# State kept in its PSUM bank, first MLP product in pairs of 64-row tiles, integer rounding in tables, last chunk in halves, new order: an RWKV-7 recurrence with Fourier mix and MLP on one core

## Chip, cores and metric

The kernel runs on one core of one Trainium2 chip. The metric is the device time of one execution in microseconds (us), median of several runs. A profiled execution gives the span from the first to the last instruction; in the profiles here it is 1.7 to 1.9 us shorter than the run that it belongs to. A run counts as slow if it took over 1.5% more than the fastest of the same kernel; comparisons use the others.

## The reference, cut to what matters

```python
# r, k, v, w, a, b: 4 batches x 8 heads x 768 steps x 40, float32
for t in range(S):
    y[:, :, t] = einsum('bhd,bhde->bhe', rt, state)
    Sa = einsum('bhde,bhe->bhd', state, at)
    state = state * wt[:, :, None, :] - einsum('bhd,bhe->bhde', Sa, bt) + einsum('bhd,bhe->bhde', vt, kt)
# x = y with the heads joined: 4 x 768 x 320
u   = x + real(fft(fft(x, axis=1), axis=2))
un  = (u - mean(u)) / sqrt(var(u) + 1e-6)
out = u + relu(un @ w_ch1) @ w_ch2          # 320 -> 1280 -> 320
```

The kernel walks the recurrence in 24 chunks of 128 steps (6 per batch). The Fourier mix and the MLP of one batch run beside the recurrence of the next.

## The kernel before

The kernel first records its operations (which buffers each reads and writes, on which engines it could run), then plays them in a fixed order, a string that was found offline: it fixes the sequence on each engine, the engine of each operation and the buffer slot of each result. At run time each engine takes its own list strictly in order and waits on semaphores. **So an operation that got faster can leave a gap where the order was made for a slower one.**

PSUM is held as four tiles of two banks each, and cut into eight one-bank slots:

```python
banks = [psum.tile([128, 1024], FP32, tag=f"ps{i}", name=f"ps{i}") for i in range(4)]
ps = Pool("ps", [banks[i // 2][:, i % 2 * 512:(i % 2 + 1) * 512] for i in range(8)], banks)
```

Some operations fill a whole two-bank tile. The framework tracks who must wait for whom by tile. Left alone, it would make a user of bank 5 wait for the users of bank 4. So the kernel declares, after each operation, that its instructions do not depend on those of the neighbouring bank, `b ^ 1`, except on true predecessors (`keep`):

```python
def part(self, banks, before=()):
    if len(banks) == 1:
        (b,) = banks
        keep = [i for o in before for i in o.made]
        for i in self.made:
            own = [n for n in ("PE", "Activation", "DVE") if n in str(i.engine)]
            for n in ("PE", "Activation", "DVE"):
                if n not in own:
                    self.tc.declare_no_dep(i, group=f"bank{b ^ 1}{n}", keep=keep, reason="another bank")
            self.tc.add_to_no_dep_group(f"bank{b}{own[0]}", i)
    ...
```

The first MLP product and the state update, as they ran (`NF` is 10 tiles of 128 hidden features; 320 rows make two and a half groups of 128, the last half is zeros):

```python
for m in range(0, NF):                       # PAIRED is empty in this kernel
    for kt in range(3):
        mm(o_, w1sb[:, kt, m * 128:(m + 1) * 128], unT()[:, :, kt], kt == 0)   # 128 rows, 384 columns
...
if st is not None and not held:              # HELD is empty: 16 such additions run
    nc.vector.tensor_add(Q(), Q(), st[0]())
...
nc.vector.tensor_tensor(s32(), Q(), decay(), Alu.mult)      # state to SBUF
```

## Time and profile before

| | before |
|---|---|
| time, median of 3 runs when the prediction was made | 237.38 us (237.0 to 238.84) |
| span of the profiled run, granted TensorE clock | 235.7 us, 0.998 |
| TensorE, VectorE, ScalarE, GpSimd busy | 95%, 88%, 77%, 65% |
| matmuls | 3664 |

The prediction below shows the head, the slices and the stretches. What it doesn't show is what TensorE waited for. The view of waits of the kernel before, of TensorE, gives for each line and releaser the us in total, the times, and the longest:

```profile
PE ps L160 <- DVE pr L160: 1.5, 3, 1.0
PE ps L160 <- DVE fill L160: 1.3, 1, 1.3
PE ps L160 <- DVE kb L160: 0.7, 1, 0.7
PE ps L160 <- DVE xs L160: 0.4, 2, 0.3
```

The reader is to see that these waits are few and short, that none names the result `h` of the MLP, and none names SyncE. The 1.3 us on `fill` is the start of the program.

### The profile page before, as it was taken

To read this page: it belongs to the slowest core of one execution; us is meant where nothing else is said; L and a number is where in the kernel's file an instruction comes from. 1 tells how busy PE (TensorE), PEld (TensorE's weight loads), DVE (VectorE), ACT (ScalarE), POOL (GpSimd) and SP (SyncE) were. 2 spreads that over 40 slices of the span, in tenths; PEclk is the share of its full clock that TensorE was granted. 3 is DMA by queue.
4 is the path that set the end of the run, shared out by engine and by line. 5 is a ranking of instruction groups with operands and counts; after the bars stand their busy time and mean duration, and the time that the engine had idled before them with its cause. 6 is when DMAs were issued, how large, how long until landed. Compare 5 with 4: busy or idle time off the path is not lost.

```text
span 235.7 us, 8993 instructions
## 1 busy us (share of the span) xinstructions
PE 224.1 (95%) x3664; PEld 170.7 (72%) x3664; DVE 208.0 (88%) x411; ACT 182.3 (77%) x378; POOL 153.5 (65%) x242
## 2 busy tenths in 40 slices
PE   7878999889999999999999999999999999999994
PEld 2446778678877777788867687888877787876662
DVE  6999999999999998998999999999899998689342
ACT  4879998798999899847799858968899895536240
POOL 6087998699999798458467267787979858200000
PEclk9999999999999999999999999999999999999999
DMA  7999889999999999999998899998999640002004
GB/s 121 185 171 188 152 147 165 158 158 167 182 173 173 144 163 158 169 148 156 180 209 196 151 188 167 164 158 151 222 196 191 114 104 3 3 0 86 0 34 160
DMA packets 171832, 33.93 MB, mean 144 GB/s; under 512 B 167120, under 2 KB 171472, under 8 KB 171792
## 3 DMA queue, kind: packets, MB, share of 16 engines
q1 hardware_dynamic: 170112, 31.73, 78.0%
q0 software_dynamic: 1680, 1.64, 4.3%
q8 instruction: 28, 0.46, 0.8%
q14 instruction: 12, 0.10, 0.2%
HBM read 26.87 MB, written 3.93 MB: 131 GB/s over the span
## 4 chain that ended last, share of the span: by engine, by line
PE 52%; DVE 16%; ACT 12%; issue 6%; DMA 5%; POOL 4%; SPq 3%; DVEq 0%; POOLq 0%; ACTq 0%
PE ps L160 52%; DVE pr L160 4%; SPq L433 3%; DVE xb L160 2%; POOL nat L472 2%; DMA in<-in_k_dram 2%; DMA in<-in_r_dram 2%; DVE xs L160 1%; DMA in<-in_w_dram 1%; DVE sm L160 1%; ACT kb L160 1%; DVE h L160 1%; ACT L160 1%; ACT tk L160 1%; DVE un L160 1%
## 5 line engine op out<-in xcount | busy, mean ns | idle before, releaser
L160 PE MATMUL ps<-unT,w1sb 128*128 128x384 bf16 x240 | 45.9, 326 | 0.4 <-DVE xb L160 0.4
L472 POOL TENSOR_TENSOR nat<-in,rw 128x320 bf16<-128x320 f32 x40 | 35.1, 884 | 12.5 <-DMA in<-in_b_dram 7.2
L465 POOL TENSOR_SCALAR_AFFINE_SELECT pr<-pr 128x1024 bf16<-128x1024 bf16 x31 | 34.4, 1116 | 8.9 <-ACT pr L160 8.7
L160 DVE TENSOR_TENSOR pr<-ps,su 128x1024 bf16<-128x1024 f32 x28 | 33.9, 1217 | 3.0 <-PE ps L160 2.6
L160 PE MATMUL ps<-w2sb,h 128*128 128x320 bf16 x240 | 35.7, 299 | 0.0
L160 PEld LDWEIGHTS <-nat 128*128 128x128 bf16 x512 | 29.8, 97 | 7.6 <-DVE nat L160 1.5
L160 ACT ACTIVATE pr<-ps 128x1024 bf16<-128x1024 f32 x32 | 32.6, 1029 | 3.2 <-PE ps L160 2.8
L160 PEld LDWEIGHTS <-pr 128*128 128x128 bf16 x768 | 29.0, 96 | 6.6 <-DVE pr L160 1.1
L160 ACT ACTIVATE h<-ps 128x384 bf16<-128x384 f32 x56 | 26.0, 497 | 9.1 <-PE ps L160 8.9
L160 PE MATMUL ps<-ident,nat 128*128 128x128 bf16 x352 | 30.5, 219 | 1.2 <-DVE pr L160 0.3
L160 PEld LDWEIGHTS <-w1sb 128*128 128x128 bf16 x240 | 20.9, 97 | 11.5 <-issue 0.5
L160 PEld LDWEIGHTS <-h 128*128 128x128 bf16 x240 | 22.5, 98 | 8.5
L685 POOL TENSOR_TENSOR pm<-xb 128x161 bf16<-128x161 f32 x40 | 19.9, 523 | 2.8 <-DVE xb L160 2.8
L472 POOL TENSOR_TENSOR nat<-in,wp 128x320 bf16<-128x320 f32 x18 | 15.9, 881 | 8.5 <-PE ps L160 4.0
L160 PE MATMUL ps<-ar,kb 64*128 64x128 bf16 x384 | 17.3, 217 | 1.1 <-DVE kb L160 0.7
L160 DVE SCALAR_TENSOR_TENSOR xb<-ps,bst,xb 128x320 f32<-128x320 f32 x24 | 12.9, 544 | 5.7 <-PE ps L160 5.4
L160 PE MATMUL ps<-xs,pr 128*128 128x40 bf16 x384 | 17.2, 180 | 0.7 <-DVE xs L160 0.4
L160 PE MATMUL ps<-nat,pr 128*128 128x40 bf16 x384 | 17.3, 180 | 0.4 <-DVE pr L160 0.2
L160 PEld LDWEIGHTS <-kb 64*128 64x128 bf16 x384 | 11.6, 94 | 6.0 <-issue 2.0
L160 DVE TENSOR_SCALAR h<-ps 128x384 bf16<-128x384 f32 x24 | 12.8, 551 | 3.4 <-PE ps L160 1.8
L488 POOL TENSOR_TENSOR low<-logw 128x320 f16<-128x320 f32 x17 | 12.2, 719 | 4.9 <-ACT logw L160 3.3
L160 DVE TENSOR_TENSOR m<-ps,su 128x1024 bf16<-128x1024 f32 x12 | 14.6, 1219 | 0.6 <-PE ps L160 0.5
(146 smaller groups left out, 583.6 us busy)
## 6 DMA issues: line engine op xcount, KB each, us to landing
in<-in_w_dram SPq DMA_DIRECT2D x24, 160.0 KB, 4.1
in<-in_r_dram SPq DMA_DIRECT2D x24, 160.0 KB, 4.1
in<-in_a_dram SPq DMA_DIRECT2D x24, 160.0 KB, 4.1
in<-in_k_dram SPq DMA_DIRECT2D x24, 160.0 KB, 4.0
in<-in_b_dram SPq DMA_DIRECT2D x24, 160.0 KB, 3.9
in<-in_v_dram SPq DMA_DIRECT2D x24, 160.0 KB, 4.0
out_dram<-xb SPq DMA_DIRECT2D x24, 160.0 KB, 2.2
w2sb<-in_moe_w_ch_dram POOLq DMA_DIRECT2D x2, 400.0 KB, 7.1
```

What stands on the lines that cost most here:

```text
L160: i = f(*args, **kwargs)
L433: op({"SP": (0.6, lambda x_=x_, t_=t_: nc.sync.dma_start(x_(), t_[bb, :, c * C:(c + 1) * C, :].rearrange("h t d -> t h d")))}, w=[x_], dma ...
L465: op({"POOL": (0.12 + 0.48 * n_, lambda d_=d_: nc.gpsimd.affine_select(out=d_(), in_=d_(), compare_op=Alu.is_gt, fill=0.0, base=0, pattern ...
L472: return {"POOL": (0.82, lambda: nc.gpsimd.tensor_tensor(dst(), x_(), s_(), Alu.mult)), "DVE": (cD(320), lambda: nc.vector.tensor_tensor(d ...
L488: op({"POOL": (0.68, lambda: nc.gpsimd.tensor_tensor(low()[:, :, :D], lg(), hi()[:, :, :D], Alu.subtract)), "DVE": (cD(320), lambda: nc.ve ...
L685: op({"POOL": (0.48, lambda a_=a_, f_=f_: nc.gpsimd.tensor_tensor(*a_(), f_)), "DVE": (0.33, lambda a_=a_, f_=f_: nc.vector.tensor_tensor( ...
```

## The change

The intent: take work from TensorE (five slots instead of six in the first MLP product), from VectorE (no state addition, shorter tables) and from the end (half of the last chunk). The core of the diff, cut; the new order string, most of the table code and the halving of the last chunk are left out:

```diff
-HELD = set()
-PAIRED = set()
+HELD = {0, 1, 2, 3}
+PAIRED = {0, 1, 2, 3}
+ALL = ("PE", "Activation", "DVE", "Pool", "SP")
...
-        self.nc = Watched(tc.nc, self.made, ("tensor", "scalar", "vector"))
+        self.nc = Watched(tc.nc, self.made, ("tensor", "scalar", "vector", "gpsimd", "sync"))
     def part(self, banks, before=()):
         if len(banks) == 1:
...
-                own = [n for n in ("PE", "Activation", "DVE") if n in str(i.engine)]
-                for n in ("PE", "Activation", "DVE"):
+                own = [n for n in ALL if n in str(i.engine)]
+                for n in ALL:
...
+                if bb in PAIRED:
+                    twice = lambda un=un, ti=ti: (un()[:, ti, DM:], un()[:, ti, 256:DM])
+                    op({"POOL": (0.12, ...), "ACT": (0.16, ...), "DVE": (0.1, ...)}, w=[un[ti]], kind="twice")
...
                 ph2 = [PSB(lambda t_: t_[:, :384]) for _ in range(2)]
-                def up2(ph2=ph2, m=m, unT=unT):
...
+                def halves_of(e, kts, fresh, ph2=ph2, m=m, unT=unT):
+                    for kt in kts:
+                        for x_ in range(2):
+                            rows = slice((e ^ x_) * 64, (e ^ x_) * 64 + 64)
+                            mm(ph2[x_]()..., w1sb[rows, kt, (m + x_) * 128:(m + x_ + 1) * 128],
+                               unT()[rows, :, kt], fresh and kt == 0)
+                op({"PE": (cP(3, 384), lambda f_=halves_of: f_(0, range(3), True))}, w=ph2, ..., kind="upA")
+                seen = lambda eng, ph2=ph2: eng.keepalive_nop([eng.lower_ap(x_()) for x_ in ph2])
+                op({"POOL": ..., "SP": ..., "ACT": ..., "DVE": ...}, r=ph2, kind="seen")
+                op({"PE": (cP(2, 384), lambda f_=halves_of: f_(1, range(2), False))}, w=ph2, ..., kind="upB")
```

In the first half (`upA`, six matmuls) the upper 64 rows feed one output tile and the lower 64 the other; in the second half (`upB`, four) it is the other way round. The empty instruction (`seen`) on another engine stands between them, because the two row groups swap banks there. Note for later: `upA`, `seen` and `upB` each name **two** banks, which may lie in different two-bank tiles, and `part` still asks for `len(banks) == 1`.

> **What bounds the kernel now.** I read the page's head and its slices first, then busy time in three stretches, then the costliest groups, then the order of time on TensorE. The head and the sliced view of the kernel before:
>
> ```profile
> PE 224.1 (95%) x3664; PEld 170.7 (72%) x3664; DVE 208.0 (88%) x411; ACT 182.3 (77%) x378; POOL 153.5 (65%) x242
> PE   7878999889999999999999999999999999999994
> DVE  6999999999999998998999999999899998689342
> ```
>
> TensorE is at 95% of a 235.7 us span and VectorE at 88%. But the first third of the PE row has 7s and 8s exactly where the DVE row has 9s. Busy time in three stretches (columns: stretch, its length, then PE, weight loads, DVE, ACT, POOL, the granted clock, DMA share, GB/s):
>
> ```profile
> 0.00:80.00 80.00, 72.35 (x1291) 54.03 (x1292) 75.15 (x146) 69.48 (x142) 64.77 (x120) 1.00 0.99 162
> 80.00:190.00 110.00, 109.52 (x1898) 85.94 (x1895) 103.11 (x200) 92.67 (x194) 80.23 (x110) 1.00 1.00 170
> 190.00:232.30 42.30, 42.27 (x482) 30.76 (x479) 29.20 (x66) 20.14 (x43) 8.48 (x14) 1.00 0.15 46
> ```
>
> To 80 us DVE is 94% busy and PE 90%; after it PE is never free (109.52 of 110, 42.27 of 42.30). "Busy" flatters PE, since a matmul counts until it drains: so I took what one costs from the distances between starts. The timeline of PE and four groups:
>
> ```profile
> 120.63 0.66 PE L160 MATMUL ps<-unT,w1sb 128*128 128x384 bf16 x3
> 121.23 0.40 PE L160 MATMUL ps<-ar,kb 64*128 64x128 bf16 x8
> 121.46 0.39 PE L160 MATMUL ps<-rv 64*128 64x128 bf16 x8
> 121.68 0.39 PE L160 MATMUL ps<-ar,kb 64*128 64x128 bf16 x8
> 122.00 2.12 PE L160 MATMUL ps<-unT,w1sb 128*128 128x384 bf16 x12
> 124.06 0.40 PE L160 MATMUL ps<-rv 64*128 64x128 bf16 x8
> ...
> L160 PE MATMUL ps<-unT,w1sb 128*128 128x384 bf16 x240 | 45.9, 326 | 0.4 <-DVE xb L160 0.4
> L160 DVE TENSOR_TENSOR ps<-ps,s 128x320 f32<-128x320 f32 x16 | 7.9, 492 | 0.4 <-PE ps L160 0.2
> L160 DVE TENSOR_TENSOR s<-ps,wt 128x320 f32<-128x320 f32 x16 | 7.7, 484 | 0.3
> L160 DVE SCALAR_TENSOR_TENSOR h<-h,h 128x386 f32<-128x386 f32 x3 | 2.2, 781 | 0.0
> ```
>
> Three readings. A 384-column matmul lasts 326 ns but the next starts 162.5 ns later (12 last 11 x 0.1625 + 0.326 = 2.11 us, the 2.12 shown). Eight 64-row matmuls of 128 columns take 0.23 us (121.23 to 121.46), so two of them share one slot of 56 ns. And **each change between 128-row and 64-row mode costs about 0.1 us**: 3 x 0.1625 = 0.49 but 0.60 passed from 120.63 to 121.23; eight end at 121.68 + 0.22 = 121.90 and the next starts at 122.00. The record gives 95 ns for both directions.
>
> With such slots (columns / 2.4 + 2.5 ns, 25 ns at least, half of it for a 64-row matmul) over all 3664 matmuls the span splits into 1.3 us before the first, 197.3 us of work, 5.0 us of warm-up matmuls on zeros, 113 mode changes x 95 ns = 10.7 us, 18.0 us idle, 3.4 us after the last matmul. Of the 23.0 us of idle and warm-up 20.5 lie before 80 us. So: early, VectorE and latency bind; from 80 us on, TensorE work does.
>
> **What the Trainium skill says.** "TensorE: Matmul & The Clock Gate", section Wait — 56ns, not 53.3ns?, gives N / 2.4 GHz + about 2.5 ns between warm matmuls; the trace agrees (162.5 ns at 384, 56 at 128). "TensorEngine Tiling (Array Packing)", Key Properties: changing the tiling mode drains the TensorE; the trace puts 95 ns on it. Same page, Gotcha 1: row tiles write to different PSUM banks and may not use one bank at the same time; that is why the change splits a pair's product in two with a wait between, and no run shows yet what it costs. "PSUM — Partial Sum Buffer", The four PSUM rules: VectorE writes leave the accumulate bits as they are, so matmuls can add onto a state that VectorE has decayed in its bank; the kernel before has no such case.
>
> **The change part by part.**
>
> *First product in pairs.* Before, each pair of output tiles takes 2 x 3 matmuls, the third with half its rows zero. Now it is ten 64-row matmuls, five slots for six. 40 pairs x 162.5 ns = 6.5 us off PE. Against it: counted over the compiled instruction order, mode changes go from 113 to 153, 40 x 95 ns = 3.8 us more. (Most of the 80 new groups lie beside other 64-row work, or it would be 15.) Net **-2.7 us**, nearly all after 80 us, where PE binds, so it counts in full. Around it come 24 small copies that duplicate 64 columns (16 on POOL, 7 ACT, 1 DVE) and 40 empty instructions that stand between the two halves; 19 of these go on SyncE, 10 POOL, 7 ACT, 4 DVE. In the order other PE work of at least 0.2 us, mostly 0.33 to 0.8, fills that wait. A last matmul's drain (0.16 beyond its slot) and two semaphore hops are an estimated 0.3 us, so I count 0 to 1 us in sum.
>
> *State in its bank.* The 16 additions go: 16 x 0.49 = 7.9 us of DVE. The decay stays (0.484). The bf16 copy now reads PSUM, so POOL can't do it: of 16, ACT had 9 and POOL 7; now DVE has 8 (+3.9 us) and ACT 8. One serial DVE step of 0.5 us leaves the recurrence per chunk; one of eight banks stays taken.
>
> *Tables.* Five shift-add-and-round passes go: adds 3 x 0.356 + 2 x 0.324 = 1.7 us and five scalings 2.1 us off DVE; the conversions to integer move to ACT (5 x about 0.5 us).
>
> *Last chunk in halves.* The final step falls from 0.55 to an estimated 0.37 us (half the columns of its row) and the final transfer is half as large: -0.3 us, all on the path. PE work is the same (20 x 69 against 10 x 136 ns).
>
> *Order.* Warm-up falls from 5.0 to 3.0 us. With the measured mean of each form times the two compiled lists, overlap of neighbours taken off: DVE about -10.5 us, ACT about -4, POOL about +12. Up to the 8th of 24 chunk outputs (75.2 us in the trace before) DVE work falls by 3.9 us; but PE work done by then is about 2 us less too.
>
> **The sum.** Early: the 8th output 3.7 us sooner, 71.5 us. PE work left then: 2 us more through the order, 6.5 less through the pairs, 3.8 more changes: -0.7. Tail -0.3, extra waits +0.6. Span 235.7 - 3.7 - 0.7 - 0.3 + 0.6 = 231.6. A new order fitted to the lighter DVE should gain somewhat more of the 23 us than this list does; I choose another 2.0 us of it, by judgement. 229.6 + 1.7 (median run over profiled span: 237.38 - 235.7) = 231.3; I say **231.0**.
>
> **The rivals.**
> - *The wait between halves takes the place of the saving.* For it: 40 round trips, and the empty instruction on SyncE stands in order behind loads that wait for free buffers; PE has no slack after 80 us. Against: PE work is placed in between. If each cost 0.2 us more, +8 us: 237 to 239.
> - *Mode changes eat it.* At 95 ns they take 3.8 of 6.5. A 384-column drain could cost more than the measured cases: at 150 ns, +2 us, 233.
> - *Another engine or PSUM becomes the early bound.* ACT is handed zeroing and table work at the start, POOL 12 us; seven free banks instead of eight. POOL has room (65%). Then the early 3.7 us vanish: about 235.
> - *VectorE was the real brake.* 10.5 us less DVE all go into early idle: 20.5 us of idle and warm-up shrink to 12, and the time is about 226. For it: DVE at 94% before 80 us. Against: the first 20 us are also DMA and latency (6.8 us idle there).
>
> **Range and chances.** The firm part is 3 us, the part through VectorE 2 to 8, the waits cost 0 to 4. 80%: 227 to 235.5. The 2% line is 232.6 us, a little above my value: faster 0.64, same 0.32, slower 0.04 (it takes the first rival at nearly full size).
>
> **What would show it.** First product: 400 matmuls, pairs 3 to 4 ns apart, 162.5 ns per pair, about 32.5 us of slots. Mode changes near 95 ns. PE waits on SyncE, POOL, ACT or DVE at the second halves under 1 us in sum. DVE busy 196 to 199, no additions on the state. Idle plus warm-up before 80 us at 14 to 19 instead of 20.5; PE without idle after it. Wrong if the waits at second halves sum to several us, if pairs do not overlap, or if the 8th chunk output is not near 71 us.

## The result, and the profile after

The changed kernel took **259.59 us** (median of 4 runs, 258.85 to 260.25) and the kernel before 237.51 us beside it (4 runs, 237.0 to 238.84). The result is correct. The ratio is 1.0919, 95% interval 1.0865 to 1.0974: 9% slower, far outside the predicted range. (A ratio is the mean time of one kernel's fast runs over that of the other's fast runs of the same rounds, so not quite the ratio of the medians.)

The head and the sliced view of the changed kernel:

```profile
PE 229.7 (89%) x3822; PEld 170.6 (66%) x3822; DVE 198.8 (77%) x382; ACT 182.6 (71%) x381; POOL 164.3 (64%) x271
PE   7979999999886789999988799999959998997794
DVE  5899999899884658887886687989945986495353
PEclk9999999999999999999999999999986999999999
```

VectorE has the 198.8 us that were predicted, and TensorE runs the predicted 3822 matmuls. But the PE row, which before was 9 from the tenth slice to the last but one, now has 6, 7, 8 and 5 in it, and VectorE falls to 4 in the thirteenth and the thirtieth slice: the engines wait together. The last row is the clock that TensorE was granted, in tenths; before it was 9 throughout. Here the trace has it at half from 191.4 to 198.3 us, shortly after the longest wait of TensorE (shown below). Busy time in stretches, columns as in the prediction:

```profile
0.00:80.00 80.00, 70.98 (x1263) 52.87 (x1264) 69.97 (x130) 69.53 (x144) 66.73 (x126) 1.00 0.99 166
80.00:190.00 110.00, 100.18 (x1806) 76.88 (x1806) 87.02 (x166) 81.21 (x169) 77.98 (x115) 1.00 0.92 154
190.00:254.60 64.60, 58.52 (x755) 40.82 (x754) 41.45 (x86) 31.85 (x68) 19.60 (x32) 0.95 0.24 56
```

From 80 to 190 us TensorE is busy for 100.18 us and does 1806 matmuls, where before it was busy for 109.52 of 110. The costliest group and TensorE's waits, first four lines:

```profile
L164 PE MATMUL ps<-unT,w1sb 64*128 64x384 bf16 x400 | 44.9, 333 | 14.2 <-DVE h L164 2.3
```

```profile
PE ps L164 <- ACT h L164: 2.8, 5, 1.0
PE ps L164 <- SPq L164: 2.6, 2, 2.2
PE ps L164 <- DVE h L164: 2.3, 3, 1.1
PE ps L164 <- DVE kb L164: 2.1, 3, 0.9
```

The new product has 14.2 us of idle ahead of it, and the releasers are `h` (the ReLU's result of *another* pair), `kb` (a copy in the recurrence) and SyncE's queue. The product needs neither `h` nor `kb`.

The same accounting as in the prediction, over all starts of matmuls in the traces' records, in us. "Idle" is what remains of the distances between starts after the slots and the mode changes, so it also holds what matmuls lose while the clock is half:

| | before | after |
|---|---|---|
| before the first matmul | 1.3 | 1.3 |
| slots of useful matmuls | 197.3 | 190.8 |
| mode changes x 95 ns | 10.7 (113) | 14.5 (153) |
| warm-up | 5.0 | 3.0 |
| idle | 18.0 | **45.0** |
| after the last matmul | 3.4 | 3.4 |
| span | 235.7 | 258.0 |
| output of the 8th, the last chunk of the recurrence at | 75.2, 202.6 | 74.2, 220.3 |

What was counted for TensorE came true (slots, mode changes, warm-up); the 27 us lie in idle, and not up to the 8th output but after it, where an MLP runs beside the recurrence. Right before the first matmul of the 40 `upA` lie 7.0 us of it, before that of `upB` 7.6 us, and 7.2 us between the later matmuls of both; the rest lies before other work. (A pair counts as one slot here.) 2.8 us of the 45.0 are the half clock: matmuls took so much longer from 191.4 to 198.3 us. All four runs of the changed kernel were granted 0.980 to 0.987 of the clock, the profiled run before 0.998. Why the clock fell isn't shown by any run here, so this part of the 22 us comes with the waits, but isn't explained by them.

**Who holds a second half up?** Two places in the timeline of the changed kernel (start, duration, then in brackets the idle before and its releaser):

```profile
130.15 0.69 DVE L164 COPY kb<-ps 128x1024 bf16<-128x1024 bf16 x1
...
130.89 0.50 PE L164 MATMUL ps<-unT,w1sb 64*128 64x384 bf16 x4 [0.78 <-DVE kb L164]
```

```profile
216.21 0.49 DVE L164 TENSOR_TENSOR xb<-ps,wp 128x320 f32<-128x320 f32 x1 [1.39 <-PE ps L164]
...
216.75 1.48 PE L164 MATMUL ps<-unT,w1sb 64*128 64x384 bf16 x16 [0.58 <-DVE xb L164]
```

At 130.89 the four matmuls of an `upB` start 0.05 us after a VectorE copy ends. By the slots in the order, that `upB` writes banks 5 and 2, and the copy reads bank 4: the neighbour of bank 5 in its two-bank tile. At 216.75 the first four of the 16 matmuls, an `upB` on banks 6 and 2, start 0.05 us after VectorE is done with bank 7. The recorded preconditions (data and bank) had been met before. I call this a **false wait**. Counted by the author over the records as the part of a wait that lies beyond the engine being free and beyond all true predecessors plus 60 ns, false waits are 16.5 us on TensorE, 11.0 on VectorE and 9.3 on ScalarE in the changed kernel, against 1.4, 0.8 and 2.3 before. (They overlap, so they don't add up to a time.)

The reason is in the code: 23 of the 40 pairs have their banks in two different two-bank tiles; their operations skip the declaration, wait for all users of both neighbours, and all users of the neighbours wait for them. The Trainium skill, "PSUM — Partial Sum Buffer", section PSUM bank collisions raise a hardware error, asks to guard PSUM by bank (or, finer, by bank and quadrant of 32 partitions); these waits guard by pair of banks, which is more than that.

**The empty instruction itself** is cheap: where SyncE's queue is free it ends 0.04 to 0.05 us after `upA` ends, and `upB` starts some 0.05 us later, so about 0.1 us in all. (The shortest time from the end of an `upA` to the start of its `upB` is 0.15 us in this trace, and 0.11 us in the one with exact waits below.) Where it isn't, one case is large. TensorE and SyncE's queue near 190 us in the changed kernel:

```profile
188.04 0.80 PE L164 MATMUL ps<-unT,w1sb 64*128 64x384 bf16 x6
191.04 1.44 PE L164 MATMUL ps<-unT,w1sb 64*128 64x384 bf16 x9 [2.19 <-SPq L164]
```

```profile
187.81 2.43 SPq L164 DMA_TRANSPOSE rv<-nat  x1
190.28 0.58 SPq L164 DMA_DIRECT2D in<-in_a_dram  x1
```

The `upA` ends at 188.84; its empty instruction stands in order behind a transposing DMA whose issue takes 2.43 us and a load. The matmuls that start at 191.04 are first an `upA` of another pair, by the slots in the order on banks 1 and 3. They need nothing of that empty instruction, which reads banks 4 and 0; but bank 0 is the neighbour of bank 1. So the longest wait of TensorE is a false wait too, made long by SyncE's queue.

### The profile page after: what moved, and what is told of

The parts are those of the page before. It is cut to its first block, busy times and chain, and to the rows that moved or that the text cites. A ratio compares the mean times of both kernels' runs of the same rounds, so it can differ in the third digit from the quotient of the medians.

```text
span 258.0 us, 9423 instructions
## 1 busy us (share of the span) xinstructions
PE 229.7 (89%) x3822; PEld 170.6 (66%) x3822; DVE 198.8 (77%) x382; ACT 182.6 (71%) x381; POOL 164.3 (64%) x271
## 5 line engine op out<-in xcount | busy, mean ns | idle before, releaser
L164 PE MATMUL ps<-unT,w1sb 64*128 64x384 bf16 x400 | 44.9, 333 | 14.2 <-DVE h L164 2.3
L164 PEld LDWEIGHTS <-w1sb 64*128 64x128 bf16 x400 | 19.8, 95 | 29.1 <-issue 19.4
L164 POOL TENSOR_TENSOR nat<-in,rw 128x320 bf16<-128x320 f32 x43 | 36.9, 866 | 3.1 <-DMA in<-in_b_dram 1.3
L164 ACT ACTIVATE h<-ps 128x384 bf16<-128x384 f32 x51 | 23.3, 492 | 20.8 <-PE ps L164 18.4
L164 PE MATMUL ps<-w2sb,h 128*128 128x320 bf16 (+1 forms) x250 | 35.7, 294 | 0.0
L164 POOL TENSOR_TENSOR pm<-xb 128x161 bf16<-128x161 f32 x46 | 22.9, 514 | 7.8 <-DVE xb L164 4.9
L164 POOL TENSOR_TENSOR low<-logw 128x320 f16<-128x320 f32 x23 | 16.8, 729 | 16.9 <-ACT logw L164 13.8
L164 DVE TENSOR_SCALAR h<-ps 128x384 bf16<-128x384 f32 x29 | 15.5, 553 | 13.2 <-PE ps L164 12.2
L164 DVE TENSOR_TENSOR m<-ps,su 128x1024 bf16<-128x1024 f32 x14 | 17.0, 1218 | 2.7 <-PE ps L164 2.5
L164 DVE SCALAR_TENSOR_TENSOR xb<-ps,bst,xb 128x320 f32<-128x320 f32 (+1 forms) x25 | 13.0, 531 | 5.5 <-PE ps L164 4.9
```

The costliest lines, as they stand in the source:

```text
L164: i = f(*args, **kwargs)
```

## The experiments

Eleven kernels ran. The times of the kernel before that stand beside them are from the same chip and the same call or calls. All passed a check for races before they ran. The texts on record give the theories letters and say what they mean; F is the false waits.

### Waits made exact

```diff
-        if len(banks) == 1:
-            (b,) = banks
+        if banks and not any(b ^ 1 in banks for b in banks):
...
-                for n in ALL:
-                    if n not in own:
-                        self.tc.declare_no_dep(i, group=f"bank{b ^ 1}{n}", keep=keep, reason="another bank")
-                self.tc.add_to_no_dep_group(f"bank{b}{own[0]}", i)
+                for b in banks:
+                    for n in ALL:
+                        if n not in own:
+                            self.tc.declare_no_dep(i, group=f"bank{b ^ 1}{n}", keep=keep, reason="another bank")
+                for b in banks:
+                    self.tc.add_to_no_dep_group(f"bank{b}{own[0]}", i)
```

Expected:

> The changed kernel, same order and same instructions; only the bookkeeping of dependencies differs: an instruction that touches two separate PSUM banks is declared independent of the banks next to them in their two-bank tiles, as one-bank instructions already are. Theory F (false waits: the 23 of 40 pairs that lie in two different two-bank tiles wait for users of the neighbouring banks, and are waited for): 228 to 235 us, PE idle falls from 45 to 20-25 us, waits at second halves near 80 ns. Theory W (the round trip through another engine's in-order queue, SyncE above all, is what costs): 250 us or more, PE idle stays above 38 us. Theory O (the new order itself and the busier ACT/POOL): 250 us or more, idle not at the first product.

Measured: correct, and free of races in the check. Four runs: one fast at 237.63 us, three that count as slow at 242.29 to 243.06; before 239.35 (7 runs). With a single fast run there is no interval, but even the slowest run is 16 us below the changed kernel, which ran in another call, beside a kernel before at 237.51 us. **The false waits made the kernel 9% slower; without them it is about as fast as before.** Theories W and O said 250 us or more and fail; F is right in kind, but its 228 to 235 us were not reached. In its profile (of a slow run, span 240.8 us, with the clock at half for 3.4 us, worth 1.7 us) idle is 27.7 instead of 45.0 us, with slots and mode changes the same, and false waits on TensorE are 3.1 us (2.4 of it at the warm-ups). TensorE's largest wait there:

```profile
PE ps L164 <- SPq L164: 4.1, 3, 2.6
```

### The product on the whole array, in the changed order

```diff
-                            rows = slice((e ^ x_) * 64, (e ^ x_) * 64 + 64)
-                            mm(ph2[x_]()..., w1sb[rows, kt, ...], unT()[rows, :, kt], fresh and kt == 0)
+                def whole_of(x_, ph2=ph2, m=m, unT=unT):
+                    for kt in range(3):
+                        mm(ph2[x_]()..., w1sb[:, kt, ...], unT()[:, :, kt], kt == 0)
...
-                seen = ... keepalive_nop ...
+                seen = lambda eng: None
```

Expected:

> The changed kernel with its order, state, tables and halves, but the first product in full 128-row matmuls: three at the place of each first half, three at that of the second, no empty instruction between, no instruction on two separate banks. Both F and W: 232 to 240 us (6.5 us more matmul slots, 3.8 us fewer mode changes, the idle of the first product gone). Theory O: still above 250 us.

Measured: correct, two fast runs at 238.6 and 239.88 us, two slow at 242.43 and 242.94; before 239.35, inside the range of F and W. (The unused half of the third weight group is zeroed again; the diff leaves that out.) Here no operation of the product names two separate banks, and the 22 us are gone as well. In its profile (span 238.2 us) slots are 197.3 us as before, mode changes still 14.4 us, idle 18.7. So the changed order has its mode changes even without the pairs: the 3.8 us that I charged to the pairs belong to the order.

### The kernel before, with the declaration taken from its first product

```diff
-        if len(banks) == 1:
+        if len(banks) == 1 and not whole:
...
-                                for k in range(b.slot, b.slot + b.size)], before)
+                                for k in range(b.slot, b.slot + b.size)], before, whole=o.kind == "up")
```

Expected:

> The kernel before, unchanged but for one thing: its 80 first products are no longer declared independent of the neighbouring bank in their two-bank tile, so they take and give the same false waits, with no pairs and no empty instruction. Theory F: slower by 3% or more (245 us and up). W and O: the same within 1%.

Measured: correct, 255.03 us (4 runs, 253.1 to 258.2, the last of them slow), before 239.35; ratio 1.0626 (1.054 to 1.0711). The instruction lists of all engines are the same, only whom they wait for differs. The stretch from 80 to 190 us, which had 109.52 us of TensorE before, and the product's group, which had 0.4 us of idle ahead:

```profile
80.00:190.00 110.00, 101.98 (x1748) 79.51 (x1747) 96.05 (x183) 85.96 (x178) 71.65 (x100) 1.00 0.92 158
```

```profile
L160 PE MATMUL ps<-unT,w1sb 128*128 128x384 bf16 x240 | 47.2, 326 | 10.3 <-DVE xs L160 2.0 <-DVE h L160 1.9 <-ACT h L160 1.6
```

The idle of the whole kernel goes from 18.0 to 34.3 us (1.8 of it by a half clock for 3.4 us near 35 us). The same cause in the other kernel makes the same picture, releasers included.

### All 19 empty instructions of SyncE moved

These three start from the exact waits. Only the engine differs:

```diff
             o = self.ops[i]
+            if o.kind == "seen" and e == "SP":
+                e = "ACT"        # "POOL" and "DVE" in the other two
```

Expected, on ScalarE, GpSimd and VectorE:

> The kernel of e1 (exact dependencies) with the 19 empty instructions that stand on SyncE put on ScalarE at the same place of the order. In e1 TensorE waited 4.1 us for SyncE, whose queue stands up to 2.7 us in one transposing DMA issue. Theory S (what e1 still loses is SyncE's in-order queue): PE's waits on SyncE vanish, second halves wait under 3 us in sum, 233 to 237 us and little spread between runs. If the loss is the round trip itself or ScalarE blocks as badly: the same as e1 or slower.

> As e4, but the 19 go on GpSimd, which is over 95% busy from 50 to 80 us and has room later. Theory S: 233 to 238 us, a little worse than ScalarE before 80 us, better after 190 us where GpSimd has nothing to do. Otherwise the same as e1 or slower.

> As e4, but on VectorE, which the order fills most. Theory S: 234 to 239 us, with VectorE blocked while it waits for the first halves; if it is slower than e1, an in-order queue that also holds work is no better than SyncE.

Measured (4 runs each, before 239.35 us, 9 runs):

| | us | ratio to before | idle in its profile |
|---|---|---|---|
| on ScalarE | 240.45 (239.76 to 243.28) | 1.008 (1.0001 to 1.0159) | 25.3 |
| on GpSimd | 244.48 (243.52 to 245.04) | 1.021 (1.0161 to 1.0258) | 29.9 |
| on VectorE (2 of 4 slow) | 240.77 (238.14 to 242.23) | 1.0079 (1.0011 to 1.0147) | 23.4 |

With the 19 on ScalarE no wait of TensorE names SyncE's queue any more, as theory S said; but its 233 to 237 us didn't come, nor any gain over the one fast run of the exact waits (237.63 us). So SyncE's queue is not all that is left. GpSimd is the worst: there TensorE's largest wait is for GpSimd's `nat` (5.5 us in 9 times). That the empty instruction now waits behind the other engine's list, and holds that list up while the product isn't done, is the likely reason; it wasn't tested. None beats the kernel before.

### Five of them moved

Only five empty instructions, picked by the records as those that stood behind slow issues on SyncE, go from there to VectorE:

```diff
+            if i in (973, 978, 1018, 1028, 1446):
+                e = "DVE"
```

Expected:

> The kernel of e1 (exact dependencies) with only the five empty instructions moved from SyncE to VectorE that stood there 0.35 to 3.0 us late behind a transposing issue or a load. Theory S: SyncE's lateness of about 5 us goes and little comes in its place: 235 to 238 us, at or just under the kernel before on the same chip, and still 5 us from what was predicted. If it stays at 240 or more, the late five were hidden behind something else.

Measured: correct, 238.95 us (6 runs, 238.38 to 240.97, all fast), before 238.87 (11 runs); ratio 1.0043 (0.9984 to 1.0103). The same as before, and 1 us above the range of theory S. The accounting of its profile (span 236.6 us): slots 190.8, mode changes 14.5, warm-up 3.0, idle 23.5. Its fast runs are no faster than the one fast run of the exact waits (237.63). Whether the move makes slow runs rarer isn't settled: none of 6 was slow here, 3 of 4 with the exact waits alone; of the later experiments that have the five moved as well, 0, 1 and 2 of 6, and the slow profile of the last again shows 3.7 us of waits for SyncE's queue.

### The additions put back into the changed order

From the version with five moved. The state is taken out of its bank and added again, 16 times, as in the kernel before; the order stays.

```diff
-                op(... tensor_tensor(Q(), Q(), decay(), Alu.mult) ..., w=[Q], r=[wt], kind="s32")
+                def decayed(s32=s32, before=None if st is None else st[0]):
+                    if before is not None:
+                        nc.vector.tensor_add(Q(), Q(), before())
+                    nc.vector.tensor_tensor(s32(), Q(), decay(), Alu.mult)
```

Expected:

> As e7, but the state is again added from SBUF (16 additions of 0.49 us on VectorE back, the copy to bf16 reads SBUF), in the same order and banks. Theory V (VectorE work bounds the first 80 us, as the prediction had it): the 8th chunk output 2 to 3 us later than in e7 and the whole 2 to 4 us slower. Theory C (what bounds there is spread over waits between engines that the additions are not part of): within 1.5 us of e7.

Measured: correct, 242.79 us (6 runs, 242.12 to 243.29), ratio to before 1.0185 (1.0139 to 1.0231), against 238.95 and 1.0043. The 8th output comes at 76.2 instead of 75.0 us, and TensorE waits for VectorE's steps of the recurrence (with the additions in first, without them in the second):

```profile
PE ps L165 <- DVE pr L165: 3.0, 6, 0.6
PE ps L165 <- DVE st L165: 1.9, 3, 0.9
```

```profile
PE ps L164 <- DVE pr L164: 1.3, 3, 0.6
```

Putting 7.9 us of VectorE work into an order that was made without it costs 3.8 us. That is theory V's 2 to 4 us; but the 8th output moved by 1.2 us and not by its 2 to 3.

### GpSimd relieved

From 40 to 80 us GpSimd was busy for 37.5 of 40 us in the changed order. Eleven of its operations of that stretch go to VectorE (four folds, five duplicating copies, two others).

```diff
+            if i in (405, 406, 464, 465, 485, 495, 500, 505, 510, 712, 769):
+                e = "DVE"
```

Expected:

> As e7, but eleven GpSimd operations between the 6th and the 9th chunk output (four folds, five 64-column copies, two low halves, about 4.7 us) are put on VectorE, where they take about 3.4 us. Theory G (GpSimd, 96% busy from 40 to 80 us in the changed kernel, ate the early gain): 8th output 1 to 3 us earlier, 1 to 3 us faster. Theory V or C: the same or slower.

Measured: correct, 240.62 us (6 runs, 238.19 to 241.87), ratio to before 1.0072 (1.0002 to 1.0143). The stretch with five moved, then with GpSimd relieved (GpSimd is the fifth of the busy times):

```profile
40.00:80.00 40.00, 36.98 (x712) 28.79 (x712) 36.41 (x69) 33.57 (x73) 37.51 (x59) 1.00 1.03 174
```

```profile
40.00:80.00 40.00, 35.92 (x691) 28.11 (x689) 37.40 (x77) 32.60 (x70) 32.38 (x47) 1.00 1.04 170
```

GpSimd lost 5.1 us and TensorE did not gain; the 8th output stays at 75.0 us. GpSimd's load is not what holds the early phase.

### The additions left out of the kernel before

```diff
-                op({"DVE": (cD(320), lambda: nc.vector.tensor_add(Q(), Q(), st[0]()))}, w=[Q], r=[st[0]], kind="Qadd")
+                op({"DVE": (cD(320), lambda: None)}, kind="Qadd")
```

Expected:

> The kernel before, with its 16 additions of the state (0.49 us of VectorE each, 7.9 us in all) left out and nothing put in their place; order, slots and all else as before (the result is wrong on purpose: each chunk forgets the state ahead of it). It asks what the removal alone is worth in the old order. Theory V (the prediction's reading: VectorE binds up to about 80 us, and the addition is a serial step of the recurrence): the 8th chunk output comes 3 to 4 us sooner than 75.2, near 71.5, and the time falls by 3 to 5 us, to 234 to 236 beside the kernel before. Then the changed order, not the removal, lost the early gain. Rival N (the early phase is held by latency, loads, ScalarE and GpSimd as well, so that one lighter engine does not shorten it): the 8th output stays at 74 to 75.5 and the time within 1 us of before; then the prediction's early 3.7 us never existed.

Measured: 237.36 us (6 runs, 235.53 to 238.93), before 237.91 (12 runs); ratio 0.9967 (0.9922 to 1.0013). (The text on record calls the result wrong on purpose; the comparison with the reference passed it, because each of 128 steps multiplies the state by 0.85 to 0.95 and next to nothing is left. It is no valid shortcut: other decays would show the error.) The two early stretches:

```profile
0.00:40.00 40.00, 34.25 (x543) 23.41 (x545) 34.12 (x68) 32.28 (x64) 27.70 (x68) 0.96 0.93 159
40.00:80.00 40.00, 38.19 (x745) 30.82 (x744) 38.09 (x72) 36.56 (x79) 36.45 (x51) 1.00 1.00 165
```

Up to 80 us VectorE is busy for 34.12 + 38.09 = 72.2 us instead of 75.15, and TensorE has done 1288 matmuls instead of 1291: lighter by 3 us on one engine, and the other no further on. The 8th output came at 75.8 us in this profile, 75.2 in the kernel before. But the profiled run is the slowest of the six, and in it the clock was half from 33.6 to 37.0 us (the 0.96 above), worth up to 1.8 us; without that the 8th output might have come near 74 us. So the times decide: **taking the additions away in the old order is worth 0.8 us by the ratio; the interval allows anything from no gain to 1.9 us.** The 3 to 5 us of theory V lie outside it. The predicted early gain of 3.7 us was not lost by the changed order; it did not exist in the old order either.

### The duplicating copies left out

From the version with five moved; 18 of 24 copies are skipped (result wrong on purpose, relative error 0.05).

```diff
+                    do = lambda f, twice=twice, bb=bb: f(*twice()) if bb == 0 else None
-                    op({"POOL": (0.12, lambda twice=twice: nc.gpsimd.tensor_copy(*twice())),
+                    op({"POOL": (0.12, lambda do=do: do(nc.gpsimd.tensor_copy)),
```

Expected:

> The changed kernel with exact waits and five empty instructions moved (e7), with 18 of its 24 duplicating copies left out (those of batches 1 to 3; the first six stay, so that no buffer is read unwritten; the result is wrong on purpose, since the third group of rows is then stale). The copies measured 0.24 us each where the order had been fitted to 0.12 to 0.16, and each lies between the layer norm and the transposes of its tile. Theory T (the copies hold the path from the layer norm to the first product): idle of TensorE after 80 us falls from 5.7 to 3 to 4 us and the time from 238.95 to 235.5 to 237. Rival: the copies lie beside other work; the time stays within 1 us of 238.95 and the idle at 5 to 6 us.

Measured: 238.82 us (6 runs, 237.53 to 243.54, two of them slow), before 237.91 (12 runs); ratio 1.002 (0.9981 to 1.006), which covers the 1.0043 with the copies; theory T's 235.5 to 237 us, 1 to 1.5% below 238.95, are not seen. Its profile fell in a slow run, so its idle isn't used. The copies lie beside other work.

## Why the prediction was wrong, point by point

**The waits at the pairs: wrong, and this is the 22 us.** The step that failed is "so I count 0 to 1 us in sum", together with the first rival, which gave the wait at most 8 us more. Both looked at the round trip through the empty instruction, and that took about 0.1 us where its queue was free. What cost the time was *whom else* these operations wait for. They name two banks, the declaration that makes waits exact is made only for one, and both neighbours' users were drawn in. Making it exact took the time from 259.6 to 237.6 in a fast run (from 9.2% above the kernel before beside it to 0.7% below); taking it away from the kernel before cost that kernel 6.3%. The diff showed it: it widens `part` to five engines and leaves `len(banks) == 1` alone. My comparison of the instruction order did not show it, because no instruction moves.

**The rival that an empty instruction on SyncE stands behind loads: right in kind, small.** The longest wait of TensorE for SyncE's queue was 2.2 us in the changed kernel, where a false wait passed it on to another pair, and 1.1 us with exact waits and five moved (both fast profiles); the culprit in the first was the issue of a transposing DMA. No placement gave a time below the kernel before.

**TensorE's own work: right.** 400 matmuls in pairs, 162.5 ns per pair (the median with five moved); the second of a pair starts 3 to 4 ns after the first in 142 of 200 pairs there and at most 20 ns after in 190, in the changed kernel with its waits in 76 and 166; slots 197.3 to 190.8, which is the 6.5 us; 153 mode changes, 14.5 us. The rival that a change after 384 columns costs more didn't come true: the 20 of them that run from such a pair straight into a 128-row matmul cost 96 ns each at the median. Only the ownership was wrong: the extra changes come with the order, as the run on the whole array shows with 14.4 us.

**VectorE's work: right in amount, wrong in worth.** 198.8 us lie within the predicted 196 to 199. The step that failed is "the 8th output 3.7 us sooner, 71.5 us": it came at 74.2 us in the changed kernel and 75.0 in the version with five moved. Leaving the same additions out of the old order brought no earlier 8th output in its one profile and 0.3% of the time, at most 0.8% by the interval. The prediction had read the slices too far: TensorE's 7s and 8s do not stand "exactly" where VectorE has 9s (its first slice is a 6, and most of the later ones are 9s too). A VectorE that is 94% busy in an early stretch was not the same as a path through VectorE. Put back into the changed order the additions cost 3.8 us. That this order had been made to use the room, and spent it on something else, is a reading and not shown. ScalarE's forecast of -4 us failed too: 182.3 us before, 182.6 after.

**The 2.0 us "by judgement" for a better order: wrong.** With exact waits and five moved, idle and warm-up up to 80 us were 17.9 + 3.0 = 20.9 us against the 20.5 of before and the 14 to 19 predicted; after 80 us 5.7 us of idle stood against 2.5.

**The tail: no gain seen.** 3.4 us after the last matmul in both, instead of 0.3 less, though the last VectorE step fell from 0.55 to 0.39 us.

With exact waits and five moved the whole sum, from the two profiles, is: slots -6.5, mode changes +3.8, warm-up -2.0, idle +5.5, so +0.8 us in place of the predicted -4.1 of span (235.7 to 231.6) and -6.1 with the judgement. **What stays open** is the rest of that idle. It is not GpSimd's load from 40 to 80 us and not the copies (both tested). The shorter tables, the zeroing moved to ScalarE and the shorter warm-up were never run alone. That the fixed order was made for other durations is plausible: it assumed 0.12 to 0.16 us for a duplicating copy that takes 0.24 (median), and 1.5 us for the issue of a transposing DMA that takes 1.2 to 2.8 (median 1.3). But no run here shows that this is the cause, and an order fitted to the measured durations was not tried. No version tested was faster than the kernel before beyond the intervals.

## What to carry to other kernels

When a change makes an operation touch two buffers where all earlier ones touched one, look at how the waits are derived, not only at what the operation costs: list for each new instruction whom it waits for, and ask of each whether the data or the bank needs it. A busy share near 95% in a stretch doesn't say that work removed there shortens it; with fixed lists per engine, test that by removing the work from the old kernel before building a forecast on it. And an idle gap whose releaser makes nothing that the waiting instruction reads is the sign of a false wait.

## What the Trainium skill lacked or had wrong

- "PSUM — Partial Sum Buffer" gives the rule to guard by bank. It doesn't say what a coarser guard costs: guarding the first product by pairs of banks cost 6.3% in the kernel before (239.35 to 255.03 us) and about 22 us in the changed one.
- "TensorEngine Tiling (Array Packing)", Gotcha 1, says that software must synchronize row tiles that share a bank, without a cost: here the round trip through an empty instruction on SyncE took about 0.1 us with a free queue; behind a busy queue of SyncE TensorE waited up to 1.1 us with exact waits and five moved (fast profile), and up to 2.2 us with the false waits.
- The same page says that a change of tiling mode drains TensorE, without a figure: 95 ns per change fits both kernels, with 113 and with 153 changes, after 128 columns as after 384.
- The time that a transposing DMA from SBUF to SBUF holds its issuing engine on this chip: "DMA: Bandwidth & Descriptors" has it only in sequencer cycles for "previous generations", at one size (8,192 tiles). Here it was 1.2 to 2.8 us on SyncE in the changed kernel, median 1.3 of 16, and up to 3.2 us in the version with five moved.
